# Second batch of a linear-attention and feed-forward kernel: k-v products ahead of the turns of q, and the relu and copies of q divided between ScalarE and VectorE

## Chip, cores, metric

The kernel runs on one core of a Trainium2 chip. The metric is device time in microseconds (us), the median of several executions. Ratios are computed as the mean time of one kernel's runs over the mean of the other's of the same rounds, so they are not quite the ratio of the medians that I quote.

## The reference, cut to what matters

```python
q, k, v: (8, 8, 576, 64) float32                     # batch, heads, positions, width
phi(x)  = concat(relu(x) * cos_w, relu(x) * sin_w)   # weights by position
kv      = phi(k)^T v                                 # per batch and head
x       = phi(q) kv / (phi(q) sum(phi(k)) + 1e-6)    # to (4608, 512)
out     = (silu(x @ w_gate) * (x @ w_val)) @ w_out   # d_ff 1536
```

The 4608 rows are handled as nine groups of 512 tokens, each group being four tiles of 128. Gate, value and output products of these groups fill TensorE; the attention of the batches is threaded between them. This is about the second batch (b = 1 in the code). Its k-v products, and the turned q that is multiplied with them, are prepared at the end of the gate and value products of the first 512 tokens. Tile 4, the first of the second 512 tokens, is the first to need them.

## The kernel before

The parts that the change and the argument touch; cuts are marked.

```python
    def relu_slots(b, lo, hi):                       # relu of q, put slots-first
        ...
        relu_op("dve", st["qp"][:, b, lo:hi].rearrange("p c j (i d) -> p c (j i) d", i=2),
                raws[b, "q"][:, :, lo:hi].rearrange("p g c d -> p c g d"))

    def qturn_pe(b, j, lo, hi, eng):                 # turns of q, and the copy out of PSUM
        ps = take(1).bitcast(BF16).rearrange("p (c x) -> p c x", x=P)
        for c in range(lo, hi):
            nc.tensor.transpose(out=ps[:, c - lo], in_=st["qp"][:, b, c, j], identity=ident)
        copy_op(eng, qt_of(b)[:, :, j, lo:hi]..., ps[:, 0:hi - lo]...)

    def kv_mm(b):                                    # 72 products of 64x64 tiles into two banks
        ps = st[b, "kvps"] = take(2, ("kv", b))
        for j, c in [(j, c) for j in range(J) for c in range(NC)]:
            ...                                      # j = 0 needs groups 0, 1 of k and v; j = 1 groups 2, 3

    def kv_out(b, engs=("act", "dve"), js=slice(0, J)):   # the casts: two on ScalarE, two on VectorE
        ...
    def a_half(t, j):                                # attention of tile t: turned q times cast k-v
        ...
    at("b9", ...), at("b10", ...)                    # weightings of v (vmul), two behind block 9, two behind block 10
        if g == 2:
            at(s, lambda: relu_slots(1, 0, CUT))     # the relu of q stands ahead of the last weighting
    at("b11", q_(1, 0, 0), q_(1, 1, 0), lambda: kv_mm(1), lambda: kv_out(1))
    at((0, 0), lambda: kv_free(1), a_(4, 0), a_(4, 1))    # after the first four output products
```

Each engine carries out its instructions in the order in which this plan issues them. A turn is a transpose by TensorE into PSUM, the buffers for its results (`banks` in the profiles); a cast copies finished k-v products out of them, from fp32 to bf16. In the profiles L513 is the gate and value products, L549 the output products, L285 the k-v products, L274 the turns of q, L333 the copies of what was turned, L297 the casts of the k-v products, L444 the attention of tiles 4 to 7, L239 the weighting of v, and L220 and L218 relus on VectorE and ScalarE.

Of the kernel before, what the change touches and what calls it, by code (L numbers as in the profile page):

```python
# [18 lines left out]
def kernel(  # L19
# [14 lines left out]
    J = G // 2  # L34
# [31 lines left out]
    def take(n, hold=None):  # L66

        taken = {x for r in held.values() for x in r}
        free = [b for b in range(0, 8, n) if not any(b <= x < b + n for x in taken)]

        b0 = min(free, key=lambda b: (n == 1 and hold is not None and hold[0] == "o" and b ^ 1 not in taken,
                                      sorted(used[b:b + n], reverse=True)))
        if hold is not None:
            held[hold] = range(b0, b0 + n)
        touch(range(b0, b0 + n))
        return banks[:, b0] if n == 1 else banks[:, b0:b0 + n]
# [10 lines left out]
    raws = {}  # L87
# [22 lines left out]
    CUT = 7  # L110
# [103 lines left out]
    st = {}  # L214

    def relu_op(eng, out, in_):
        if eng == "act":
            nc.scalar.activation(out=out, in_=in_, func=AF.Relu)  # L218
        else:
            nc.vector.tensor_single_scalar(out=out, in_=in_, scalar=0.0, op=ALU.max)  # L220
# [17 lines left out]
    def vmul(b, g):  # L238
        nc.vector.tensor_tensor(  # L239
            out=v2s[b % 2][:, g, :, :, 0:D],  # L240
            in0=(first if b == 0 and g == 0 else {"v": raw_of(b, "v")})["v"][:, g].unsqueeze(2).to_broadcast([P, NC, 2, D]),
            in1=tab, op=ALU.mult,
        )
# [16 lines left out]
            in_=st[b, "q"][e * SH:(e + 1) * SH].rearrange("p g c w d -> p (g c w d)"),  # L260
        )

    def relu_slots(b, lo, hi):

        if "qp" not in st:
            both = rel.tile([P, G, NC, 2, D], BF16, name="r_q").rearrange("p g c w d -> p (g c w d)")
            st["qp"] = both.rearrange("p (b c j x) -> p b c j x", b=2, c=NC, j=J)
        relu_op("dve", st["qp"][:, b, lo:hi].rearrange("p c j (i d) -> p c (j i) d", i=2),
                raws[b, "q"][:, :, lo:hi].rearrange("p g c d -> p c g d"))

    def qturn_pe(b, j, lo, hi, eng):
        ps = take(1).bitcast(BF16).rearrange("p (c x) -> p c x", x=P)
        for c in range(lo, hi):
            nc.tensor.transpose(out=ps[:, c - lo], in_=st["qp"][:, b, c, j], identity=ident)  # L274
        copy_op(eng, qt_of(b)[:, :, j, lo:hi].rearrange("p e c s -> p c e s"),
                ps[:, 0:hi - lo].rearrange("p c (e s) -> p c e s", e=2))

    def kv_mm(b):
        ps = st[b, "kvps"] = take(2, ("kv", b))
        for j, c in [(j, c) for j in range(J) for c in range(NC)]:  # L280
            for i in range(2):
                for e in range(2):
                    es = slice(e * SH, (e + 1) * SH)
                    g = 2 * j + i
                    nc.tensor.matmul(  # L285
                        out=ps[i * D:(i + 1) * D, e, j * 2 * D1:(j + 1) * 2 * D1],
                        lhsT=raws[b, "k"][es, g, c],
                        rhs=v2s[b % 2][es, g, c, :, 0:D1],
                        start=(c == 0), stop=(c == NC - 1),
                    )  # L290

    def kv_out(b, engs=("act", "dve"), js=slice(0, J)):
        ps = st[b, "kvps"]
        for e, eng in enumerate(engs):
            for i in range(2):
                hs = slice(i * D, (i + 1) * D)
                (nc.scalar.copy if eng == "act" else nc.vector.tensor_copy)(  # L297
                    out=kvd[b % 2][hs, e, js, :, i].rearrange("p j w x -> p (j w) x"),
                    in_=ps[hs, e, js.start * 2 * D1:js.stop * 2 * D1].rearrange("p (y x) -> p y x", x=D1))
# [10 lines left out]
    def kv_free(b):  # L310
        give_back(("kv", b))
# [295 lines left out]
    def at(s, *fns):  # L607
        plan.setdefault(s, []).extend(fns)
# [5 lines left out]
    def a_(t, j):  # L614
        return lambda: (a_half(t, j), x_norm(t) if j else None)
# [4 lines left out]
    def q_(b, j, part, eng="act"):  # L620
        lo, hi = ((0, CUT), (CUT, NC))[part]
        return lambda: qturn_pe(b, j, lo, hi, eng)
# [17 lines left out]
    for word in words:  # L640
        word, _, eng = word.partition("@")
        op, a, b = re.match(r"([A-Za-z]+)(\d+)\.?(\d*)", word).groups()
# [44 lines left out]
    def turn_last():  # L687
        for j in range(J):
            qturn_pe(0, j, NC - 1, NC, "act")

    at("a8", lambda: relu_slots(0, NC - 1, NC))
    at("b9", turn_last)
    at("a8", lambda: relu_k(1, 0, 2, "dve"))
    at("a9", lambda: relu_k(1, 2, 4, "act"))
    for g, s in enumerate(("b9", "b9", "b10", "b10")):
        at(s, lambda g=g: vmul(1, g))
        if g == 2:
            at(s, lambda: relu_slots(1, 0, CUT))
    at("b11", q_(1, 0, 0), q_(1, 1, 0), lambda: kv_mm(1), lambda: kv_out(1))
    at((0, 0), lambda: kv_free(1), a_(4, 0), a_(4, 1))  # L700
    at((0, 2), a_(5, 0))
    at((0, 3), a_(5, 1))
# [10 lines left out]
    at((1, 3), a_(7, 1))  # L713
    at((2, 0), turn(6, True))
    at((0, 3), lambda: relu_slots(1, CUT, NC))
    at((2, 1), q_(1, 0, 1), q_(1, 1, 1))
    at((2, 2), turn(7, True))
# [35 lines left out]
    for t in range(2 * OUT, NTG * OUT):  # L753
        tg, i = divmod(t, OUT)
        s = SLOTS * (tg - 1) + (5 if tg > 2 else 4) + 2 * i
# [50 lines left out]
```

## Time and profile before

| | before |
|---|---|
| median of 3 runs | 325.91 us (325.68 to 326.5) |
| span of the profiled execution | 324.0 us |
| TensorE busy | 317.4 us (98%) |
| VectorE, ScalarE busy | 181.5 us (56%), 132.2 us (41%) |

A busy share of 98% tells that TensorE is the bound. What it leaves is 6.6 us, and the next view tells how much of that lies where the change acts. It is the busy time by stretch of the kernel before: the stretch in us, its length, then busy time and instruction count of TensorE, its weight loads, VectorE, ScalarE and GpSimd, and then the granted clock, the DMA share and GB/s.

```profile
20.00:38.00 18.00, 18.00 (x127) 11.95 (x126) 9.39 (x22) 8.57 (x19) 7.31 (x10) 1.00 1.35 201
38.00:44.00 6.00, 5.11 (x106) 3.06 (x105) 4.04 (x8) 3.58 (x7) 0.00 (x0) 1.00 1.27 205
44.00:56.00 12.00, 12.00 (x72) 6.36 (x71) 9.37 (x27) 5.88 (x13) 1.65 (x3) 1.00 0.91 133
```

TensorE is full on both sides and idle for 0.89 us of the six in between; the rest of the 6.6 us lies in the first 20 and the last 24 us of the span. Meanwhile VectorE and ScalarE are idle for about a third and two fifths of those six (4.04 and 3.58 busy).

### The profile page before, as it was taken

Reading aid. Unit: us, or ns where it says so; the run is one execution under the profiler, and the core shown is the slowest. Engines: PE = TensorE matmul, PEld = TensorE weight load, DVE = VectorE, ACT = ScalarE, POOL = GpSimd, SP = SyncE. Lnnn points to the kernel's source line nnn. Section 1 sums busy time; section 2 is a strip of 40 time slices with the busy share of each in tenths; the row PEclk is TensorE's granted clock in tenths of the full one; section 3 lists DMA queues with packets and bytes.
Section 4 is the critical chain, followed back from the end, with each engine's and each line's share of the span. In section 5 each row is a group of like instructions: output and inputs, shape, how many; then the busy total and the mean of one; then the engine's idle time right before and its main releaser. Section 6 shows DMA issues by size and latency. Waiting matters only on the chain.

```text
span 324.0 us, 6046 instructions
## 1 busy us (share of the span) xinstructions
PE 317.4 (98%) x2396; PEld 159.8 (49%) x2396; DVE 181.5 (56%) x362; ACT 132.2 (41%) x242; POOL 34.9 (11%) x59
## 2 busy tenths in 40 slices
PE   8899899999999999999999999999999999999995
PEld 4596455455445444544454445444554445444443
DVE  7873867786475647565657555755564236423420
ACT  7453455653553335332632354344432132213311
POOL 6845002002000200020002000200000000000000
PEclk9999999999999999999999999999999999999999
DMA  7999998999675997699778969697921411240014
GB/s 274 211 200 197 206 190 119 219 119 156 146 121 80 162 184 122 91 140 145 172 106 114 172 149 129 87 170 158 135 45 35 104 26 34 40 104 19 0 32 99
DMA packets 72748, 40.64 MB, mean 125 GB/s; under 512 B 48272, under 2 KB 67472, under 8 KB 72720
## 3 DMA queue, kind: packets, MB, share of 16 engines
q1 hardware_dynamic: 50368, 22.55, 38.3%
q0 software_dynamic: 22192, 17.57, 37.4%
q8 instruction: 19, 0.31, 0.4%
q10 hardware_dynamic: 160, 0.13, 0.1%
q14 instruction: 9, 0.07, 0.1%
HBM read 37.75 MB, written 9.44 MB: 146 GB/s over the span
## 4 chain that ended last, share of the span: by engine, by line
PE 93%; DVE 4%; ACT 1%; issue 0%; ACTq 0%
PE banks L513 57%; PE banks L549 28%; PE banks L285 3%; PE banks L399 2%; DVE v L239 1%; PE banks L444 1%; PE banks L381 1%; PE banks L485 1%; DVE raw_k L220 1%; PE banks L568 1%; DVE ht L524 0%; DVE qwT L369 0%; PE banks L274 0%; ACT L184 0%; DVE r_q L220 0%
## 5 line engine op out<-in xcount | busy, mean ns | idle before, releaser
L524 DVE TENSOR_TENSOR ht<-sg,banks 128x512 bf16<-128x512 bf16 (+2 forms) x116 | 74.7, 649 | 69.6 <-PE banks L513 63.1
L519 ACT ACTIVATE sg<-banks 128x512 bf16<-128x512 f32 (+2 forms) x116 | 65.8, 568 | 112.7 <-PE banks L513 109.7
L513 PE MATMUL banks<-xT,wv_sb 128*128 128x512 bf16 (+2 forms) x464 | 111.3, 364 | 0.0
L513 PE MATMUL banks<-xT,wg_sb 128*128 128x512 bf16 (+2 forms) x464 | 111.3, 364 | 0.0
L549 PE MATMUL banks<-wo_sb,ht 128*128 128x512 bf16 x420 | 94.3, 379 | 0.0
L513 PEld LDWEIGHTS <-wv_sb 128*128 128x128 bf16 x464 | 44.9, 98 | 48.7
L513 PEld LDWEIGHTS <-wg_sb 128*128 128x128 bf16 x464 | 43.3, 98 | 43.2
L549 PEld LDWEIGHTS <-ht 128*128 128x128 bf16 x420 | 40.2, 98 | 45.1 <-issue 0.2
L556 ACT COPY ob<-banks 128x512 f32<-128x512 f32 x18 | 10.5, 585 | 50.9 <-PE banks L549 48.9
L235 DVE TENSOR_TENSOR r_q<-raw_q,tab 128x1152 bf16<-128x1152 bf16 x24 | 17.9, 754 | 20.2 <-ACT raw_q L218 20.2
L556 DVE COPY ob<-banks 128x512 f32<-128x512 f32 x17 | 11.7, 691 | 28.3 <-PE banks L549 27.4
L239 DVE TENSOR_TENSOR v<-raw_v,tab 128x1152 bf16<-128x1152 bf16 x31 | 23.0, 752 | 0.2 <-ACT raw_v L580 0.2
L421 DVE TENSOR_TENSOR x<-banks,rec 128x512 bf16<-128x512 f32 (+1 forms) x32 | 21.6, 674 | 1.3 <-PE banks L381 0.3
L218 ACT ACTIVATE raw_k<-raw_k 128x576 bf16<-128x576 bf16 (+1 forms) x25 | 17.3, 695 | 0.0
L730 POOL COPY hold<-phit 1x2 bf16<-1x2 bf16 x5 | 0.9, 175 | 141.2 <-DMA phit<-r_q 141.2
L218 ACT ACTIVATE raw_q<-raw_q 128x576 bf16<-128x576 bf16 x24 | 15.7, 680 | 0.9 <-DMA raw_q<-in_q_dram 0.8
L399 PEld LDWEIGHTS <-phit 128*128 128x128 bf16 (+1 forms) x240 | 9.9, 100 | 6.0 <-issue 1.3
L399 PE MATMUL banks<-kv,phit 128*128 128x65 bf16 (+1 forms) x240 | 11.5, 195 | 0.0
L152 PE MATMUL banks<-zeros 128*128 128x64 bf16 (+1 forms) x64 | 9.4, 310 | 1.0 <-DVE zeros L147 1.0
L308 DVE CAST kv<-banks 64x260 bf16<-64x260 f32 x12 | 5.1, 428 | 7.4 <-ACT kv L308 7.3
L285 PEld LDWEIGHTS <-raw_k 64*64 64x64 bf16 x504 | 7.5, 106 | 2.6 <-issue 2.5
L285 PE MATMUL banks<-v,raw_k 64*64 64x130 bf16 x504 | 8.7, 218 | 0.0
(81 smaller groups left out, 134.1 us busy)
## 6 DMA issues: line engine op xcount, KB each, us to landing
out_dram<-ob SPq DMA_DIRECT2D x70, 128.0 KB, 2.4
raw_k<-in_k_dram POOLq DMA_DIRECT2D x7, 576.0 KB, 10.8
raw_q<-in_q_dram POOLq DMA_DIRECT2D x6, 576.0 KB, 7.3
raw_v<-in_v_dram POOLq DMA_DIRECT2D x6, 576.0 KB, 13.2
wo_sb<-in_moe_w_out_dram POOLq DMA_DIRECT2D x3, 512.0 KB, 12.8
wg_sb<-in_moe_w_gate_dram POOLq DMA_DIRECT2D x5, 256.0 KB, 9.8
wv_sb<-in_moe_w_val_dram POOLq DMA_DIRECT2D x5, 256.0 KB, 10.0
wo_sb<-in_v_dram SPq DMA_DIRECT2D x2, 576.0 KB, 4.1
```

The source lines that it names most:

```text
L152: nc.tensor.matmul(out=ps, lhsT=zeros, rhs=zeros[:, 0:cols].unsqueeze(1).to_broadcast([P, 4, cols]), start=True, stop=True)
L218: nc.scalar.activation(out=out, in_=in_, func=AF.Relu)
L235: nc.vector.tensor_tensor(out=st[b, "q"][:, g], in0=o.unsqueeze(2).to_broadcast([P, NC, 2, D]), in1=tab, op=ALU.mult)
L239: nc.vector.tensor_tensor(out=v2s[b % 2][:, g, :, :, 0:D], in0=(first if b == 0 and g == 0 else {"v": raw_of(b, "v")})["v"][:, g].unsqueez ...
L285: nc.tensor.matmul(out=ps[i * D:(i + 1) * D, e, j * 2 * D1:(j + 1) * 2 * D1], lhsT=raws[b, "k"][es, g, c], rhs=v2s[b % 2][es, g, c, :, 0:D ...
L399: nc.tensor.matmul(out=ps[ms, e, g * D1:(g + 1) * D1], lhsT=phit[b][:, e, g, c:c + n].rearrange("p c s -> p (c s)"), rhs=kv2s[b % 2][:, e, ...
L421: nc.vector.tensor_tensor(out=st["x", t].rearrange("p (y e d) -> p e y d", e=2, d=D)[:, :, ys], in0=ps[:, :, 0:2 * J * D1].rearrange("p e ...
L513: nc.tensor.matmul(out=st["f", tg, fc, lo][i], lhsT=(wg_sb, wv_sb)[i][:, kc, fs], rhs=xT[tg][:, ts, kc], start=(kc == 0), stop=(kc == KC - 1))
L519: nc.scalar.activation(out=sg[:, 0:n], in_=st["f", tg, fc, lo][0], func=AF.Silu)
L524: nc.vector.tensor_tensor(out=hts[tg % 2][:, fc, r:r + n], in0=st.pop(("s", tg, fc, lo))[:, 0:n], in1=ps[1], op=ALU.mult)
L549: nc.tensor.matmul(out=o_ps[t], lhsT=hts[tg % 2][:, fc, r:r + P], rhs=wo_sb[:, fc], start=(fc == 0), stop=(fc == FC - 1))
L556: (nc.scalar.copy if t % 2 == 0 else nc.vector.tensor_copy)(out=ob, in_=ps)
```

## The change

The intent is to close that idle stretch. The k-v products, which are ready earlier, go ahead of the turns. The relu of q goes behind the weighting of v, half of it on ScalarE. The second half of the turned q is copied by VectorE in place of ScalarE.

```diff
-    def relu_slots(b, lo, hi):
+    def relu_slots(b, lo, hi, js=slice(0, J), eng="dve"):
...
-        relu_op("dve", st["qp"][:, b, lo:hi].rearrange("p c j (i d) -> p c (j i) d", i=2),
-                raws[b, "q"][:, :, lo:hi].rearrange("p g c d -> p c g d"))
+        relu_op(eng, st["qp"][:, b, lo:hi, js].rearrange("p c j (i d) -> p c (j i) d", i=2),
+                raws[b, "q"][:, 2 * js.start:2 * js.stop, lo:hi].rearrange("p g c d -> p c g d"))
...
         at(s, lambda g=g: vmul(1, g))
-        if g == 2:
-            at(s, lambda: relu_slots(1, 0, CUT))
-    at("b11", q_(1, 0, 0), q_(1, 1, 0), lambda: kv_mm(1), lambda: kv_out(1))
+    at("b10", lambda: relu_slots(1, 0, CUT, slice(0, 1), "act"), lambda: relu_slots(1, 0, CUT, slice(1, 2)))
+    at("b11", lambda: kv_mm(1), q_(1, 0, 0), q_(1, 1, 0, "dve"), lambda: kv_out(1))
```

## The prediction

> **What bounds the kernel now.** I began with the page: the busy shares, then the chain that ended last.
>
> ```profile
> PE 317.4 (98%) x2396; PEld 159.8 (49%) x2396; DVE 181.5 (56%) x362; ACT 132.2 (41%) x242; POOL 34.9 (11%) x59
> PE 93%; DVE 4%; ACT 1%; issue 0%; ACTq 0%
> ```
>
> TensorE is the bound: 317.4 of 324.0 us, and 93% of the chain. A change on another engine pays only if it shortens an idle stretch of TensorE. So the second view is what TensorE waited for between 30 and 62 us, where the second batch is prepared, and the third is the chain in that stretch (start, length, what).
>
> ```profile
> PE banks L274 <- DVE r_q L220: 0.9, 1, 0.9
> ...
> 39.87 0.95 PE banks L274 x14
> 40.83 1.18 PE banks L285 x71
> 42.01 0.97 PE banks L549 x4
> 42.97 0.59 PE banks L444 x8
> 43.56 1.83 PE banks L549 x8
> ```
>
> This is the one idle stretch that the change can touch: 0.9 us, once, in front of the fourteen turns of q (L274), which waited for VectorE's relu of q (L220). After it the k-v products (L285), the first output products (L549) and the attention of tile 4 (L444) follow closely. The whole prize is therefore about 1 us, 0.3% of the time. The fourth view is the timeline of the three engines in that stretch (start, length, what, idle before).
>
> ```profile
> 37.96 1.03 PE L513 MATMUL banks<-xT,wv_sb 128*128 128x512 bf16 x4
> 39.87 0.95 PE L274 MATMUL banks<-ident,r_q 128*128 128x128 bf16 x14 [0.89 <-DVE r_q L220]
> ...
> 38.07 0.75 DVE L239 TENSOR_TENSOR v<-raw_v,tab 128x1152 bf16<-128x1152 bf16 x1
> 38.74 1.08 DVE L220 TENSOR_SCALAR r_q<-raw_q 128x1792 bf16<-128x1792 bf16 x1
> 39.73 0.75 DVE L239 TENSOR_TENSOR v<-raw_v,tab 128x1152 bf16<-128x1152 bf16 x1
> 42.15 0.87 DVE L297 CAST kvd<-banks 64x260 bf16<-64x260 f32 x2 [1.07 <-PE banks L285]
> ...
> 40.47 1.71 ACT L333 COPY phit<-banks 128x896 bf16<-128x896 bf16 x2 [1.66 <-PE banks L274]
> 42.10 0.76 ACT L297 CAST kvd<-banks 64x260 bf16<-64x260 f32 x2
> ```
>
> The reader is to see that TensorE's next user could have been issued earlier than the idle figure says. Groups of four follow each other at 0.86 us (36.23, 37.09, 37.96), so the slot after the last group opens at 37.96 + 0.86 = 38.82; it was filled at 39.87. The true hole is 1.05 us. The fourth weighting of v (L239) stood behind the relu, until 40.48.
>
> [...]
> [...]the casts of ScalarE at 42.10 start only where its copies end (42.18, with the usual overlap). This is the point on which my number turns.
> [...]the relu of turned q, 512 bf16 elements out of PSUM, took 424 ns, and a cast of only 260 fp32 elements 427 ns.[...]
> [...]
> [...] Before, the order is full, full turns, 64x64 products, full; after, full, 64x64, full turns, full: two switches either way. [...]72 products of 217 ns pass in 1.18 us.
>
> **The change, part by part.**
> (1) *k-v products first.* They need k (its relu ended at 36.25 on ScalarE) and v. The first 36 need groups 0 and 1 of v, done at 37.55, so they issue at 38.82. At 1.18/72 us each they take 0.59 us, to 39.41. The other 36 need groups 2 and 3. Group 2 ends at 38.82 as now; group 3, now directly behind it, starts at 38.74 and ends at 39.49; TensorE sees it some 0.05 us later (as 39.82 to 39.87 before). So a short wait of 0.13 us, and the products run from 39.54 to 40.13. Before they ended at 42.01.
> (2) *relu of q split.* [...] It stands behind the silu that ends near 37.06, but its data (448 KB, issued at 27.11, 10.6 us to landing) comes near 37.7; so it runs from 37.7 to 38.6 and delays the last silu (38.22 before) by some 0.4 us. That is slack: its multiplication stands behind the relu on VectorE anyway. VectorE's half starts at 39.41. 1792 elements took 1.08, 512 took 0.285; half is near 0.6, so it ends at 40.0. Both halves are there before the turns at 40.13.
> (3) *turns of q.* 14 at 0.0625 us (0.88 us): first seven 40.13 to 40.57, other seven to 41.01. No wait.
> (4) *first output products.* 4 at 0.216 us: 41.01 to 41.87. Before, the attention of tile 4 began about 42.9, so TensorE arrives 1.03 us earlier.
> (5) *what the attention of tile 4 needs.* The casts of the k-v products (L297) still stand after the copies of the turned q in the program, one copy on each engine now. ScalarE's copy started 0.60 us after its turns did before (39.87 to 40.47); now at 40.73, with 0.91 us it ends at 41.64; its two casts end 0.68 us later (42.18 to 42.86 before): 42.32. VectorE's copy starts at 40.57 + 0.60 = 41.17; [...]it ends at 41.80 and its two casts, 0.87 us begun 0.08 before that, at 42.59. The products are done at 40.13, but the casts may not pass the copies.
> (6) *sum.* TensorE is ready at 41.87 and meets the first casts at about 42.37 and VectorE's at 42.64. Five of the eight products (0.074 us each) then remain, to 43.01. Before, the next output products were issued at 43.49. The gain is 0.48 us: 1.05 won at the front, 0.13 given back to v, and roughly 0.45 in a new wait for the casts. Afterwards TensorE has no wait over 0.2 us up to 62 us, so the 0.48 passes on to the end. The bank plan shifts (products in banks 4 and 5, turns in 2 and 6), but their last readers are done by 36.7, so no new wait for a bank.
>
> 325.91 - 0.48 = 325.4 us; I say 325.5, as the three runs (325.68 to 326.5) lie a little higher in the mean.
>
> **The rivals.** *The whole prize:* if the casts are no obstacle (VectorE's copy quick, ScalarE's no longer than its turns), the gain is 0.9 to 1.05 and the time 324.9. For it: VectorE and ScalarE are both half idle in this stretch. Against it: 0.91 us of the copy on ScalarE is measured, and its casts cannot pass it.
> *The wait takes the place of the one removed in full:* [...]nothing gained, 325.9. [...]
> *ScalarE as the new bound:* q lands later than 37.7, so the relu holds the last silu and then the copies. The relu on VectorE started at 38.74 without a wait for data, so at worst ScalarE's ends near 39.65, still before the turns. It would cost nothing.
>
> **Range and chances.** The gain lies between 0 and 1.0 us by these; the runs of one kernel spread by 0.4 us either way[...]. So 324.9 to 326.2. A 2% change would be 6.5 us, over six times the only hole in reach; I see no mechanism for it.
>
> **What would show it right or wrong.** In the profile after: no wait of L274 for r_q; a wait under 0.2 us of L285 for v; a wait of L444 for the casts (kvd) of 0.4 to 0.8 us in all; VectorE's copy of 896 near 0.62 us; ScalarE's relu of q near 0.93 us and the last silu late by about 0.4; L549 following L444 at about 43.1 in place of 43.56; the stretch afterwards the same, moved. I am wrong if L444 does not wait, if VectorE's copy takes over 0.9 us, or if a new wait appears elsewhere, such as for the bank of a turn.

The forecast's sum came to a gain of 43.49 - 43.01 = 0.48 us, and so to 325.91 - 0.48 = 325.4, said as 325.5. The 0.93 us of ScalarE's relu of q (37.7 to 38.6 above) and the 0.62 us of VectorE's copy (41.17 to 41.80): the profile after shows the two at 0.95 and 0.625 us. For the first, the trace of the kernel before gives an estimate as well: ScalarE's relus of k took 1.156 us for 1152 elements and 0.674 for 576, which makes 0.94 for 896. That the casts cannot pass the copies, on which the number turns, was assumed there; the runs below show it (41.32 behind the copy, 40.34 ahead of it).

## The result

| | before | after |
|---|---|---|
| median | 325.85 us of 4 runs (325.68 to 326.5) | 325.25 us of 4 runs (325.24 to 325.3) |
| ratio | | 0.9978 (95% interval 0.9961 to 0.9996) |
| span of the profiled execution | 324.0 us | 323.3 us |
| last gate and value group of the first 512 tokens starts | 37.96 | 37.69 |
| two output groups after the attention of tile 4 start | 43.56 | 42.85 |

The time fell by 0.60 us by the medians. The last two rows divide it; the first of them is from the timeline, the second from the chain of waits. I call the distance between them **the stretch**; all that the change touches lies inside it. It fell from 5.60 to 5.16 us, by 0.44. What follows it is the same in both profiles: 324.0 - 43.56 = 280.44 us before and 323.3 - 42.85 = 280.45 after. The other 0.27 us lies ahead of the stretch, where the change altered nothing: it is there already at the first gate and value product, 16.39 against 16.12 us by the single records of the traces.

The chain of waits after (start, length, what), to be read against the one in the prediction:

```profile
38.72 1.27 PE banks L285 x70
39.98 0.51 PE banks L274 x7
...
40.52 0.91 ACT phit L333
41.42 0.27 ACT kvd L297
...
41.71 0.38 ACT kvd L297
...
42.13 0.72 PE banks L444 x7
42.85 1.83 PE banks L549 x8
```

Before, the stretch was TensorE from the turns onwards. Now the chain leaves TensorE: it goes through ScalarE's copy of the turned q (L333) and its casts (L297) and comes back at 42.13 to the attention of tile 4 (L444). The timeline of the three engines after shows why:

```profile
37.69 1.03 PE L513 MATMUL banks<-xT,wv_sb 128*128 128x512 bf16 x4
38.65 1.34 PE L285 MATMUL banks<-v,raw_k 64*64 64x130 bf16 x72
41.76 1.09 PE L444 MATMUL banks<-kvd,phit 128*64 128x260 bf16 x8
...
38.28 0.95 ACT L218 ACTIVATE r_q<-raw_q 128x896 bf16<-128x896 bf16 x1 [1.49 <-DMA raw_q<-in_q_dram]
41.32 0.76 ACT L297 CAST kvd<-banks 64x260 bf16<-64x260 f32 x2
...
39.13 0.42 DVE L220 TENSOR_SCALAR r_q<-raw_q 128x896 bf16<-128x896 bf16 x1
40.91 0.62 DVE L333 COPY phit<-banks 128x896 bf16<-128x896 bf16 x1 [0.47 <-PE banks L274]
41.45 0.86 DVE L297 CAST kvd<-banks 64x260 bf16<-64x260 f32 x2
```

The 0.89 us in front of the turns is gone. But the eight products of L444 take 1.09 us where they took 0.66: the casts, of products that were complete at 40.0, start at 41.32 and 41.45, each behind a copy on its engine. By the code the first of the eight products still belongs to the first batch and needs no new cast; it started at 41.76. The second needs both casts of ScalarE and came at 42.13, and the fourth is the first to need VectorE's. Start to start in the two timelines:

| from, to | before | after | difference |
|---|---|---|---|
| last gate and value group to the first of turns and k-v products | 1.91 | 0.96 | -0.95 |
| turns | 0.89 | 0.88 | -0.01 |
| k-v products | 1.18 | 1.27 | +0.09 |
| first output products | 0.96 | 0.96 | 0 |
| attention of tile 4 | 0.59 | 1.03 | +0.44 |
| sum | 5.53 | 5.10 | -0.43 |

(The sums are 0.07 and 0.06 below the stretch, as the chain counts a piece from where the one before it ends.)

All runs at a glance, the stretch taken from each profile in the same way:

| run | median, us | ratio to before | stretch, us |
|---|---|---|---|
| before; again | 325.85; 325.89 | | 5.60; 5.60 |
| after; again | 325.25; 325.40 | 0.9978; 0.9987 | 5.16; 5.16 |
| only ScalarE's casts first; again | 325.31; 325.38 | 0.9988; 0.9988 | 5.17; 5.16 |
| only VectorE's casts first | 325.26 | 0.9981 | 5.07 |
| both casts first; again | 325.07; 324.98 | 0.9977; 0.9974 | 4.73; 4.73 |
| both casts first, copies swapped | 324.77 | 0.9969 | 4.62 |
| both casts first, relu whole on VectorE | 325.39 | 0.9988 | 5.02 |
| turns first, work divided | 325.30 | 0.9988 | 5.22 |
| products first, both copies on ScalarE | 326.11 | 1.0005 | 5.88 |
| products first, work not divided | 326.39 | 1.0014 | 6.23 |

The 95% intervals of the ratios are some 0.0013 to 0.0019 to either side, about 0.5 us. The times tell versions apart only where they lie farther apart than that, so the verdicts below rest on the stretches and on the waits. On one chip the times agree with them in direction where the stretches differ by 0.4 us or more; smaller differences they do not settle (beside each other, 325.30 us for the turns first and 325.40 for the kernel after, though the stretch of the former is the longer).

### The profile page after: what moved, and what is told of

Same layout as the page of the kernel before. It is cut to its first block, busy times and chain, and to the rows that moved or that the text cites. A ratio compares the mean times of both kernels' runs of the same rounds, so it can differ in the third digit from the quotient of the medians.

```text
span 323.3 us, 6046 instructions
## 1 busy us (share of the span) xinstructions
PE 317.1 (98%) x2396; PEld 159.7 (49%) x2396; DVE 181.2 (56%) x363; ACT 132.2 (41%) x242; POOL 35.1 (11%) x59
## 4 chain that ended last, share of the span: by engine, by line
PE 95%; ACT 2%; DVE 2%; issue 0%; ACTq 0%
PE banks L513 58%; PE banks L549 28%; PE banks L285 3%; PE banks L399 2%; PE banks L444 1%; PE banks L381 1%; DVE v L239 1%; PE banks L485 1%; PE banks L152 1%; PE banks L568 1%; PE banks L325 0%; ACT L184 0%; ACT phit L333 0%; PE banks L274 0%; ACT ob L571 0%; DVE qwT L369 0%
## 5 line engine op out<-in xcount | busy, mean ns | idle before, releaser
L513 PE MATMUL banks<-xT,wv_sb 128*128 128x512 bf16 (+2 forms) x464 | 111.3, 365 | 0.0
L513 PE MATMUL banks<-xT,wg_sb 128*128 128x512 bf16 (+2 forms) x464 | 111.3, 365 | 0.0
L549 PE MATMUL banks<-wo_sb,ht 128*128 128x512 bf16 x420 | 94.3, 379 | 0.0
L513 PEld LDWEIGHTS <-wv_sb 128*128 128x128 bf16 x464 | 44.8, 98 | 48.8
L513 PEld LDWEIGHTS <-wg_sb 128*128 128x128 bf16 x464 | 43.2, 98 | 43.2
L549 PEld LDWEIGHTS <-ht 128*128 128x128 bf16 x420 | 40.2, 98 | 45.1 <-issue 0.2
L399 PEld LDWEIGHTS <-phit 128*128 128x128 bf16 (+1 forms) x240 | 9.9, 100 | 6.0 <-issue 1.3
L399 PE MATMUL banks<-kv,phit 128*128 128x65 bf16 (+1 forms) x240 | 11.5, 195 | 0.0
L285 PEld LDWEIGHTS <-raw_k 64*64 64x64 bf16 x504 | 7.6, 106 | 3.0 <-issue 2.5
L285 PE MATMUL banks<-v,raw_k 64*64 64x130 bf16 x504 | 8.8, 219 | 0.0
```

Source lines behind the costliest of these rows:

```text
L285: nc.tensor.matmul(out=ps[i * D:(i + 1) * D, e, j * 2 * D1:(j + 1) * 2 * D1], lhsT=raws[b, "k"][es, g, c], rhs=v2s[b % 2][es, g, c, :, 0:D ...
L399: nc.tensor.matmul(out=ps[ms, e, g * D1:(g + 1) * D1], lhsT=phit[b][:, e, g, c:c + n].rearrange("p c s -> p (c s)"), rhs=kv2s[b % 2][:, e, ...
L513: nc.tensor.matmul(out=st["f", tg, fc, lo][i], lhsT=(wg_sb, wv_sb)[i][:, kc, fs], rhs=xT[tg][:, ts, kc], start=(kc == 0), stop=(kc == KC - 1))
L549: nc.tensor.matmul(out=o_ps[t], lhsT=hts[tg % 2][:, fc, r:r + P], rhs=wo_sb[:, fc], start=(fc == 0), stop=(fc == FC - 1))
```

## The experiments

All start from the kernel after, but for the one that repeats the kernel before.

**Is the gain all in the stretch?** The kernels after and before, unaltered, once more.

> The changed kernel once more, beside the others on one chip. Stretch meant below: from the start of the last gate-and-value group of the first 512 tokens (L513) to the start of the two output groups after the attention of tile 4 (L549 x8) in the chain of waits; 5.60 us before, 5.16 after. Theory (the change gains only inside this stretch, 0.44 us): the stretch is again 5.16, and what the times differ beyond 0.44 lies in the first 15 us, where a load of k lands differently from run to run. Rival (the change also gains elsewhere): the kernel before again takes 0.6 to 0.7 us more, with the same 0.27 us of it ahead of the changed instructions in every pair of profiles.

> The kernel before, profiled once more. Theory (the 0.27 us by which the first profile of before was behind already at 37.96 is chance of the start, not the change): the stretch is 5.60 again and the last gate-and-value group may start anywhere from 37.6 to 38.3, as the eight profiles of changed versions do (37.69 to 38.28). Rival (the change moves the start): it starts at 37.96 again, within a few hundredths.

The stretches came out at 42.95 - 37.79 = 5.16 and 43.47 - 37.87 = 5.60 us, both as at first. The last gate and value group of all profiles starts between 37.69 and 38.28 (the latter in a changed version), and before, again, at 37.87. In all fourteen profiles that group starts 21.57 to 21.58 us after the first gate and value product. So the 0.27 us ahead of the stretch is scatter of the first 16 us, and the change is worth 0.44 us. That a load of k lands differently is seen in ScalarE's first relu of k, which waited for it until 8.51 us before and 9.04 after; that the 0.27 us come from it was not shown. On the chip of the first repeat the medians differed by 325.74 - 325.40 = 0.34 us, on the first by 0.60; the two lie on either side of 0.44.

**Are the casts' places in the queues the remaining wait?** Both pairs of casts go ahead of the turns and their copies.

```diff
-    at("b11", lambda: kv_mm(1), q_(1, 0, 0), q_(1, 1, 0, "dve"), lambda: kv_out(1))
+    at("b11", lambda: kv_mm(1), lambda: kv_out(1), q_(1, 0, 0), q_(1, 1, 0, "dve"))
```

> The casts of the k-v products (kv_out) placed ahead of the turns of q and their copies, all else as after. Theory (the remaining wait of the attention of tile 4 is the casts' place behind the copies on two in-order engines): the casts start when the products end, the copies follow when the turns end, tile 4 no longer waits, the stretch falls from 5.16 to about 4.65, and the time by 0.45 to 0.5 us, to about 324.8. Rival (the copies of the turned q themselves are what tile 4 needs, and are now late instead): the wait stays at 0.5 us under another name, and the time at 325.25.

> The version with both pairs of casts first once more, beside the one with the copies swapped: stretch 4.73 again and about 325.07, unless the load of the output weights lands late, in which case the first output products wait for it and the stretch is up to 0.15 us longer.

Measured: 4.73 us twice, where 4.65 had been expected. On the same chip the means of five runs were 325.03 and 325.36 for the kernel after, 0.33 us apart, less than the 0.45 to 0.5 expected and than the 0.43 of the stretch. From the chain of waits of the first of these runs:

```profile
40.34 0.38 ACT kvd L297
40.73 0.37 ACT kvd L297
41.12 0.92 ACT phit L333
42.08 0.63 PE banks L444 x8
42.72 1.83 PE banks L549 x8
```

The casts now start when the products end (40.28 in the timeline), ahead of the copy, and the attention takes 0.63 us. Their place behind the copies is shown to be the new wait. What is left of it is 0.1 us for ScalarE's copy, as the rival had it, but at a tenth of a microsecond and not at half.

**Which of the two engines holds tile 4?** The chain of the kernel after names ScalarE's casts alone. First only ScalarE's pair was moved. The helper `kv_out_one`, which casts one engine's pair, adds six lines, so that in these profiles L450 stands for L444, L555 for L549 and L339 for both copies and casts.

```diff
-    at("b11", lambda: kv_mm(1), q_(1, 0, 0), q_(1, 1, 0, "dve"), lambda: kv_out(1))
+    at("b11", lambda: kv_mm(1), lambda: kv_out_one(1, 0, "act"), q_(1, 0, 0), q_(1, 1, 0, "dve"),
+       lambda: kv_out_one(1, 1, "dve"))
```

> Only ScalarE's two casts of the k-v products moved ahead of its copy; VectorE's two stay behind its copy. Theory (both engines hold tile 4, ScalarE longest at 42.08, VectorE next at 42.31 but needed 0.15 us later): the wait shifts to VectorE's casts, the stretch falls by only 0.1 us, to about 5.05. Rival (ScalarE's casts alone hold it, as the chain of waits names them alone): the stretch falls by the same 0.5 us as with both moved.

> ScalarE's casts alone moved ahead, once more. Theory (the first time, the first output products waited 0.15 us for the load of the output weights, landed at 41.12, which hid a gain): with the load landed in time the stretch is 5.05. Rival (VectorE's casts alone set the same end): 5.17 again, with no wait of the output products.

Measured: 5.17 and 5.16 us. Neither expectation of the first run was met: there was no gain at all. In that run the load of the output weights landed at 41.12, and the first output products waited for it, so I repeated it. The second time they did not wait, and there still was no gain. The chain of the second run ends so:

```profile
42.15 0.44 DVE kvd L339
...
42.64 0.49 PE banks L450 x5
43.13 1.83 PE banks L555 x8
```

VectorE's casts end at 42.15 + 0.44 = 42.59, and five products take 0.49 us after them. In the kernel after they ended at 41.45 + 0.86 = 42.31, and 42.31 + 0.05 + 0.49 is 42.85, where its attention ended. (0.05 is the time from the end of VectorE's work to the start of the waiting product: 42.59 to 42.64 here, and 39.82 to 39.87 for its relu before.) VectorE's casts set the end there too. The counterpart followed: only VectorE's pair moved.

```diff
+    at("b11", lambda: kv_mm(1), lambda: kv_out_one(1, 1, "dve"), q_(1, 0, 0), q_(1, 1, 0, "dve"),
+       lambda: kv_out_one(1, 0, "act"))
```

> The counterpart of moving ScalarE's casts: only VectorE's two casts of the k-v products ahead of its copy, ScalarE's stay behind its copy. Theory, formed from the two runs with ScalarE's casts moved (5.17 and 5.16, no gain): in the changed kernel VectorE's casts set the end of tile 4's attention, 0.49 us before it, and ScalarE's alone would let it end 0.63 us after them, only 0.09 us sooner. So the stretch falls to about 5.07. Rival (ScalarE's casts hold it, as the chain of waits of the changed kernel names them): no gain, 5.16. Second rival (either pair moved frees most of it): 4.8 or less.

Measured: 5.07 us, as the theory had it.

```profile
42.32 0.63 PE banks L450 x7
42.95 1.83 PE banks L555 x8
```

With VectorE early, the seven products behind ScalarE's casts take 0.63 us; in the kernel after the same line showed 0.72. The 0.09 us between them was VectorE's wait, hidden inside a merged line under ScalarE's name. One pair moved gives 0 or 0.09 us, both give 0.43: two waits stood almost side by side.

**Does the order of products and turns gain by itself?** First the turns go back to the front, and all the rest stays as after.

```diff
-    at("b11", lambda: kv_mm(1), q_(1, 0, 0), q_(1, 1, 0, "dve"), lambda: kv_out(1))
+    at("b11", q_(1, 0, 0), q_(1, 1, 0, "dve"), lambda: kv_mm(1), lambda: kv_out(1))
```

> Relu split, weighting of v first and VectorE's copy kept as after, but the turns of q put back ahead of the k-v products. Theory: the turns wait for ScalarE's relu, which waits for q to land (39.23, slot open at 38.55): 0.7 us idle; then no wait for v, and the casts are not behind the copies for long: the stretch is 5.1 to 5.2, the time as after within 0.1 us. So the order of products and turns would be worth nothing by itself, given the split. Rival (the order is what gains, the split only helps): the stretch goes back toward 5.6 and the time toward 325.7.

Measured: 5.22 us, 0.06 more than after. The wait was where I had not put it:

```profile
39.17 0.56 PE L274 MATMUL banks<-ident,r_q 128*128 128x128 bf16 x7
40.20 0.56 PE L274 MATMUL banks<-ident,r_q 128*128 128x128 bf16 x7 [0.46 <-DVE r_q L220]
```

ScalarE's half was in time for the first seven turns; the other seven waited 0.46 us for VectorE's half behind the weighting of v. After the products there was no wait for the casts. So with the work divided, the order is worth 0.06 us only, in this one profile. Part of that is luck: ScalarE's relu could start 0.11 us before the last gate and value group here (38.17 against 38.28), but 0.59 and 0.21 us after it in the two profiles of the kernel after, as q landed later. With the later of these landings the first seven turns would end after VectorE's half is ready, and the stretch would be some 5.28 us (an estimate: 1.54 us from the group to the end of ScalarE's relu, 0.05 to the first turn, seven turns at 0.056, against the 1.92 after which the other seven came here). The kernel after had 5.16 with both landings.

Then the order alone, with the relu whole on VectorE and both copies on ScalarE.

```diff
-    at("b10", lambda: relu_slots(1, 0, CUT, slice(0, 1), "act"), lambda: relu_slots(1, 0, CUT, slice(1, 2)))
-    at("b11", lambda: kv_mm(1), q_(1, 0, 0), q_(1, 1, 0, "dve"), lambda: kv_out(1))
+    at("b10", lambda: relu_slots(1, 0, CUT))
+    at("b11", lambda: kv_mm(1), q_(1, 0, 0), q_(1, 1, 0), lambda: kv_out(1))
```

> Only the moves of the change: k-v products ahead of the turns, relu of q behind the weighting of v, but the relu whole on VectorE and both copies on ScalarE as before. Theory: the relu ends 1.0 us after the weighting, the turns wait some 0.3 us for it, the copies and then the casts on ScalarE follow in series; the stretch is about 6.2 us against 5.60 before, the time 326.3 to 326.5. So the reordering without the division of work is a loss. Rival (putting the ready products first gains by itself): the stretch is 5.2 or less.

Measured: 6.23 us and 326.39 us, slower than before by 0.63 us in the stretch. The new order needs the division of the work; without it, it is a loss.

**What is VectorE's copy worth?** As after, with both copies on ScalarE.

```diff
-    at("b11", lambda: kv_mm(1), q_(1, 0, 0), q_(1, 1, 0, "dve"), lambda: kv_out(1))
+    at("b11", lambda: kv_mm(1), q_(1, 0, 0), q_(1, 1, 0), lambda: kv_out(1))
```

> As after, but both copies of the turned q on ScalarE, as they were before; the casts still behind them. Theory (the casts' place in the queue is what tile 4 waits for): ScalarE's casts end near 42.9 in place of 42.08, VectorE's are early; the stretch is about 5.9 us, 0.3 longer than before the change, and the time about 326.0. Rival (ScalarE was not the holder): the stretch stays at 5.2.

Measured: 5.88 us, and one line says why:

```profile
42.97 0.63 PE L444 MATMUL banks<-kvd,phit 128*64 128x260 bf16 x7 [0.97 <-ACT kvd L297]
```

With the casts behind the copies, the copy on VectorE is worth 5.88 - 5.16 = 0.72 us, more than the whole gain.

**What is the division of the relu worth?** Both casts first, copies on both engines, but the relu whole on VectorE behind the weighting.

```diff
-    at("b10", lambda: relu_slots(1, 0, CUT, slice(0, 1), "act"), lambda: relu_slots(1, 0, CUT, slice(1, 2)))
-    at("b11", lambda: kv_mm(1), q_(1, 0, 0), q_(1, 1, 0, "dve"), lambda: kv_out(1))
+    at("b10", lambda: relu_slots(1, 0, CUT))
+    at("b11", lambda: kv_mm(1), lambda: kv_out(1), q_(1, 0, 0), q_(1, 1, 0, "dve"))
```

> Casts first and copies on both engines, but the relu of q whole on VectorE behind the weighting of v. Theory: the turns wait 0.3 us for the relu (1.08 us against 0.42 for the half), all else keeps pace; the stretch is about 4.95 to 5.0, so the division of the relu is worth some 0.3 us and the rest of the change stands without it. Rival (ScalarE's half is needed for more than that): the stretch is 5.6 or more.

Measured: 5.02 us against 4.73 with the divided relu, so 0.29 us; the turns waited 0.29 us for the relu.

**The last tenth.** Both casts first, and the copies change places: VectorE, the quicker one (0.62 us against ScalarE's 0.91), takes the half that tile 4 needs first.

```diff
+    at("b11", lambda: kv_mm(1), lambda: kv_out(1), q_(1, 0, 0, "dve"), q_(1, 1, 0))
```

> Casts first as in the fastest version so far, and VectorE (0.62 us) copies the first half of the turned q, which tile 4 needs first, ScalarE (0.91) the second. Theory: the remaining 0.1 us wait for ScalarE's copy goes, the stretch falls from 4.73 to about 4.63, the time by 0.1 us. Rival (the load of the output weights, which landed at 41.12 in the run with only ScalarE's casts moved, now holds the first output products): no gain, or a stretch that varies with that landing.

Measured: 4.62 us, and a median of 324.77 us, 0.9969 of the kernel before (0.9955 to 0.9983). Its chain is TensorE all through, and names no wait; the 0.09 us for v stays inside the line of L285 (1.27 us, where it was 1.18 before):

```profile
38.73 1.27 PE banks L285 x70
40.00 0.89 PE banks L274 x14
40.89 0.86 PE banks L549 x4
41.75 0.57 PE banks L444 x8
42.33 1.83 PE banks L549 x8
```

This is the fastest version that I ran; none of its runs (324.72 to 325.23) reaches one of the kernel before beside it (325.66 to 326.15). Against the kernel after it won 5.16 - 4.62 = 0.54 us in the stretch; the two were not timed beside each other. Against the version without the swap, timed beside it, the means of five runs are 324.89 and 325.09: in the direction of the 0.11 us of the stretches, though these runs scatter by 0.5 us.

## Why the prediction was right

It said 325.5 us, in 324.9 to 326.2, and 325.25 was measured. This range holds the 325.85 of the kernel before too, so the time alone shows little; that the mechanism was right is shown by the stretch, the waits and the experiments. Its gain of 0.48 us is to be held against the 0.44 of the stretch. The 0.60 of the medians contains scatter of the start that no step had foreseen. Step by step:

- *The hole of 1.05 us.* Measured 0.95. The k-v products began at 38.65, though the slot opened at 37.69 + 0.86 = 38.55. The 0.10 us between the last full product and the first 64x64 one I had counted in the wrong place. It is what a change of tile form costs here (below), and the kernel before has it between its last turn and its first k-v product: they start 0.149 us apart where turns follow each other at 0.056. So the 0.0625 us a turn of the prediction, and the 0.88 us for fourteen, contain it. In the second profile of the kernel after the turns took 0.79 (40.02 to 40.81). The two errors cancel.
- *Wait for v, 0.13 us.* Measured 0.09 (1.27 against 1.18).
- *The relu on ScalarE*, said 0.93 us, took 0.95. It waited for q until 38.28, later than the 37.7 that I expected, and the last silu started 1.45 us after its group (39.14 - 37.69) where it had been 0.26 (38.22 - 37.96): 1.19 us late, not 0.4. The third rival was therefore nearer to happening than I had said. It cost nothing, as argued: VectorE stood 0.19 us for that silu, ahead of work that was not yet due.
- *VectorE's half of the relu*, said 0.6 us, took 0.42. That step was mis-sized: I took the time to go with the elements. Whole, 1792 elements took 1.08 us; half, 896 took 0.42, so half of the elements cost 39% of the time. The later relu of 2 slots, 512 elements, took 0.285 us. The three differ in shape too (whole, the trace has the destination as one run of 1792 and the source with 7 slots outermost; half, both have 7 outermost), and no run changed the shape alone, so the cause was not shown. The step was off the path, so the sum did not suffer.
- *VectorE's copy*, said 0.62 us, took 0.625. The rival with a slow copy is out; a copy of over 0.9 us was the sign of being wrong.
- *The new wait, some 0.45 us.* Measured 0.44 in the first profile and 0.53 in the second (42.89 - 41.77 = 1.12, against 0.59 before). That the first met the forecast so closely is luck. In it the first output products stood some 0.10 us for the load of their weights, which was issued at 29.23 and landed at 40.76 (issued at 28.55 in the second), and so came later to the casts; that also made the turns 0.88 us, as forecast. A new wait elsewhere was among the signs of being wrong; this one cost nothing, as the casts set the end and the stretch is 5.16 in both. The prediction also had TensorE come to tile 4 after 0.86 us of output products; it took 0.96, with another change of tile form, and this too went into the wait. The cause of the wait is shown by moving the casts (5.16 to 4.73). Its division was right in kind: ScalarE's casts first, VectorE's after, and VectorE's ending the wait. I drew the wrong conclusion from it afterwards, when I expected 0.1 us from moving ScalarE's pair alone; the true margin was the other way round, 0.09 us for VectorE's pair. The term that was mis-sized in the prediction itself is the work left after VectorE's casts: 0.37 us said, 0.49 measured.
- *The whole prize* as a rival: not with this change. With both casts first and the copies swapped, it was there: 5.60 - 4.62 = 0.98 us.
- *All of it passes on to the end.* Yes: 280.44 and 280.45 us after the stretch.

The 0.10 us ahead of the first k-v product need not stay open, for the trace of the kernel before has many changes of tile form, and products of one line in both forms. The products of L399 (attention of later tiles) start 0.216 us after the full product of L513 before them where they are full themselves (18 times) and 0.309 us where they are 128x64 (3 times); L285 behind L513 is at 0.309 us six times. The way back costs as much: a full product of L513 comes 0.033 us after a full one of L399 and 0.127 us after one of 128x64. The 1.18 us of the k-v products before contains the way back: their last one starts at 41.79, and the first output product 0.151 us later. What causes the 0.09 us was not shown.

## What to carry to other kernels

When an idle stretch of the bound engine is closed, ask at once what its next work needs, and where those instructions stand in the queues of the other engines; here casts of products complete at 40.0 stood behind copies until 41.32 and 41.45 and took back 0.44 of the 0.95 us won. Place on each engine, in its order, what is ready first, and what is needed first, ahead of the rest, and give the quicker engine the part that is needed first (the swapped copies: 4.73 to 4.62 us). When a wait has two holders a tenth of a microsecond apart, the chain names one of them, and only moving both shows the gain.
